# When the experts' weights are loaded: sixteen chunks ahead of the first tokens, the rest behind the experts' up-projections

## The chip, the core and the metric

The kernel runs on one core of one Trainium2 chip. The metric is device time in microseconds (us) of one execution, inputs and outputs in HBM. All of the work is in float32; TensorE's score matmuls take the fp32r form.

## What is computed

Attention with query pooling, and then a mixture of experts on its result. Cut to what matters:

```python
def _attn_ref(q, k, v):                 # q, k, v: 2 x 8 x 1152 x 64
    q_pool = q.reshape(B, H, S // 2, 2, D).mean(axis=3)
    scores = scale * np.matmul(q_pool, k.transpose(0, 1, 3, 2))
    attn = softmax(scores)              # written out in the reference
    return np.matmul(attn, v)

def _moe_ref(x, w_gate, w1, w2, capacity):   # x: 1152 x 512, 8 experts, F 1024, capacity 288
    logits = x @ w_gate
    expert_idx = np.argmax(logits, axis=1)
    gate_w = softmax(logits)[np.arange(N), expert_idx]
    # token i goes to the next free row of its expert while there is one
    h = np.maximum(np.einsum('ecd,edf->ecf', disp, w1), 0.0)
    y = np.einsum('ecf,efd->ecd', h, w2)
    out[i] = gate_w[i] * y[expert_idx[i], pos[i]]     # for the tokens that were kept
```

## The kernel before

**Attention** runs over eight pairs of heads (`rounds`, L686). PE makes scores (L371), transposes the exponentials (L409) and multiplies with the values (L434); the results are turned into token rows in `x_tok`, an SBUF tile of 1152 rows. `routing` (L488) picks each token's expert and scatters its row with an indirect DMA from Pool (L551) into `xs`, a buffer in HBM with 288 rows for each expert. The last five of these scatters come at the very end of attention. Behind them PE runs eight warm-up matmuls (L763, two passes each) on a tile that is already there.

**The expert stage** (L961 to L978) runs the eight experts in order. The order of the instructions is the written one on Pool, SP, ScalarE and PE (`manual_schedule(engines=MS)`).

- Tokens: `load_x(e)` (L791) brings the 288 rows of an expert from `xs` in three DMAs, into one of three buffers; for expert 0 SP issues them, for the others Pool. They can start when all scatters have landed. `trans_x` (L797) turns a block of 128 rows on PE.
- Units: an expert's rows are worked in up to four units of 64, 64, 128 and 32 rows. `unit(e, 0)` always runs. `later(e, 1)` (L948) is a branch (L950) on PE, ScalarE, VectorE and Pool, nested for the units behind it: each unit runs when the expert has that many tokens. SP has no part in the branches. Code of units that don't run is jumped over; `hint` marks for the engine, ahead of time, where a branch will be.
- A unit of 64 rows: 32 up-projection matmuls on PE (`up`, L890), ReLU on ScalarE and VectorE (L897, L895), two pairs of transposes (L904), 32 down-projection matmuls (L930), scaling on ScalarE (L822) and an indirect DMA to the output from Pool (L828). Units of 128 rows go through `block` (L849, L864).
- Weights: each expert has four chunks of 1 MB, two of `w1` and two of `w2`, 32 in all. `load_w(i)` (L608) loads chunk i from SP into buffer i mod 16 of `wraw`. Buffers 0 to 5 (`NR0`) have memory of their own and are loaded early in attention. Buffers 6 to 15 (L781) take over memory of attention's tiles, tile by tile: a load waits until the tiles under its buffer have been read for the last time. Chunks 6 to 12 (`NR1` is 13) go out before the tokens of expert 0, in the order of SP's queue, chunks 13 to 15 behind them. After expert e the four chunks from 4e + 16 follow, into the buffers that this expert has just given back.
- From chunk 15 on (`NR1 + AHEAD`) SP first reads a word of the chunk two before (L616), so that it waits until that one has landed: at most two loads are under way.

The instructions' own code is fetched by DMA as well: the page shows two queues of that kind, q8 with 32 packets of 16 KB and q14 with 25 smaller ones.

Of the kernel before, what the change touches and what calls it, by code (L numbers as in the profile page):

```python
# [20 lines left out]
EL = 3  # L21
PTB = (1, 1)
MS = {mybir.EngineType.Pool, mybir.EngineType.SP, mybir.EngineType.Activation, mybir.EngineType.PE}
NR, NR0, NR1 = 16, 6, 13
NX = 3
AHEAD = 2
ENG = [mybir.EngineType.PE, mybir.EngineType.Activation, mybir.EngineType.DVE, mybir.EngineType.Pool]
FAR = 1.0e6
UT = 2


def f32(ap):
    return ap.bitcast(F32)
# [3 lines left out]
def attention_moe(ctx: ExitStack, tc, cap, q, k, v, wg, w1, w2, out):  # L37
    nc = tc.nc
    B, H, S, D = q.shape
    SQ = S // 2  # L40
    E, DM, F = w1.shape
# [27 lines left out]
        out=upper, in_=f32(upper), compare_op=ALU.is_gt, fill=0.0, base=0,  # L69
# [20 lines left out]
    for j in range(2):  # L90
        nc.scalar.dma_start(
            out=wgi[j * D:(j + 1) * D, :, P + j * E:P + (j + 1) * E], in_=wg_r[j]
# [507 lines left out]
    wraw = [wraw_p.tile([P, 4, 512], F32, name=f"wraw{i}") for i in range(NR0)]  # L600
# [4 lines left out]
        for c in range(2):  # L605
            chunks.append((e, 1, c))

    def load_w(i):  # L608
        e, m, c = chunks[i]
        if m == 0:  # L610
            src = w1[e].rearrange("(a p) f -> p a f", p=P)[:, :, c * 512:(c + 1) * 512]
        else:
            src = w2[e, c * 512:(c + 1) * 512, :].rearrange("(a p) d -> p a d", p=P)
        if i >= NR1 + AHEAD:

            nc.values_load_multi_w_load_instructions(  # L616
                wraw[(i - AHEAD) % NR][0:1, 0, 0:1].bitcast(I32), engines=[mybir.EngineType.SP],
                skip_runtime_bounds_check_because="the value is not used",
            )
        nc.sync.dma_start(out=wraw[i % NR], in_=src)  # L620

    def posts_run(f):
        while f is not None:
# [167 lines left out]
    def load_x(e):  # L791
        q = nc.gpsimd if e else nc.sync
        for s, c in blocks:
            r = e * cap + s
            q.dma_start(out=xes[e % NX][0:c, s // P, :], in_=xs[r:r + c, :])

    def trans_x(e, b):  # L797
        xe, xf = xes[e % NX], xfs[e % 2]
        c = blocks[b][1]
        ps = tr_ps.tile([P, 512], F32, tag="tr", name="xps")  # L800
        for d in range(DC):
            nc.tensor.transpose(ps[:, d * c:(d + 1) * c], xe[0:c, b, d * P:(d + 1) * P], ident[0:c, 0:c])
        nc.scalar.copy(xf[:, :, b * P:b * P + c], ps[:, 0:DC * c].rearrange("p (d c) -> p d c", c=c))

    def tags(e, u):
        o, n = units[u]
        xe, gt, it = xes[e % NX], gts[e % 4], ids[e % 4]
        src, b = slice(o % P, o % P + n), o // P
        for g in range(1 if n == P else 2):
            rows = slice(g * n, (g + 1) * n)  # L810
            c = DM + 1 if n == P else DM + 2 + g
            nc.gpsimd.tensor_copy(gt[rows, u:u + 1], xe[src, b, DM:DM + 1])
            nc.gpsimd.tensor_copy(it[rows, u:u + 1], xe[src, b, c:c + 1].bitcast(I32))

    def send(e, u, ps):
        n = units[u][1]
        w = DM if n == P else DM // 2
        c = n * DM // w
        gate = gts[e % 4][0:c, u:u + 1]
        yo = y_p.tile([P, DM], F32, tag="yo", name="yo")  # L820
        if n >= D:
            nc.scalar.activation(yo[0:c, 0:w], ps[0:c, 0:w], AF.Copy, scale=gate)  # L822
        else:
            yq = y_p.tile([D, 256], F32, tag="yq", name="yq", bufs=1)
            nc.scalar.copy(yq[0:c], ps[c:2 * c, 0:256])
            nc.vector.tensor_tensor(out=yq[0:c], in0=ps[0:c, 0:256], in1=yq[0:c], op=ALU.add)
            nc.vector.tensor_scalar(out=yo[0:c, 0:w], in0=yq[0:c], scalar1=gate, scalar2=None, op0=ALU.mult)
        ins = nc.gpsimd.indirect_dma_start(  # L828
            out=out.rearrange("t (g d) -> (t g) d", d=w),
            out_offset=bass.IndirectOffsetOnAxis(ap=ids[e % 4][0:c, u:u + 1], axis=0),  # L830
            in_=yo[0:c, 0:w],
            in_offset=None,
            bounds_check=NTOK * DM // w - 1,
            oob_is_err=False,
        ).ins
        tc.declare_no_dep(ins, group="send", reason="each token has a row of its own")
        tc.add_to_no_dep_group("send", ins)
# [29 lines left out]
    def unit(e, u, between=(), hint=lambda: None):  # L867

        tags(e, u)
        o, n = units[u]  # L870
        if n == P:
            return block(e, u, between, hint)
        xf = xfs[e % 2]
        raw = [wraw[(4 * e + c) % NR] for c in range(4)]
        G = P // n
        Q = F // G // 256
        todo = list(between)

        def step():
            if todo:  # L880
                todo.pop(0)()

        def up(q):
            ps = h_ps.tile([P, 512], F32, tag="h", name="hps")
            for d in range(DC):
                if q and d == UT and not todo:
                    turn(0)
                for g in range(G):
                    c = g * (F // G) + q * 256
                    at = nc.tensor.matmul(  # L890
                        ps[g * n:(g + 1) * n, 0:256], xf[:, d, o:o + n], raw[c // 512][:, d, c % 512:c % 512 + 256],
                        start=d == 0, stop=d == DC - 1,
                    )
            if q:
                nc.vector.tensor_scalar_max(hs[:, q], ps[:, 0:256], 0.0)  # L895
            else:
                nc.scalar.activation(hs[:, q], ps[:, 0:256], AF.Relu)  # L897
            with tc.issue_after(at.ins):
                hint()

        def turn(q):
            ps = tr_ps.tile([P, 512], F32, tag="tr", name="htp")
            for j in range(2):
                nc.tensor.transpose(ps[:, j * P:(j + 1) * P], hs[:, q, j * P:(j + 1) * P], ident)  # L904
            dst = ht[:, 2 * q:2 * q + 2].rearrange("p j c -> p (j c)")
            if q or Q == 1:
                nc.vector.tensor_copy(dst, ps[:, 0:256])  # L907
            else:
                nc.scalar.copy(dst, ps[:, 0:256])  # L909

        held = Q == 2 and bool(todo)
        for q in range(Q):
            up(q)
        if held:
            turn(0)
        step()
        if held:
            turn(1)
        if Q == 1:
            turn(0)  # L920
        ps = y_ps.tile([P, 512], F32, tag="y", name="yps")
        U = G // 2
        NF = FC // U
        for i in range(NF):
            for w in range(U):
                j, g = divmod(i, 2) if U == 1 else (i % 2, 2 * w + i // 2)
                r = g * (F // G) + j * P
                for c in range(2):
                    k = (2 * w + c) * n
                    nc.tensor.matmul(  # L930
                        ps[k:k + n, 0:256], ht[:, j, g * n:(g + 1) * n],
                        raw[2 + r // 512][:, r % 512 // P, c * 256:(c + 1) * 256],
                        start=i == 0, stop=i == NF - 1,
                    )
            if i == 1 and Q == 2 and not held:
                turn(1)
            if i > 1:
                step()
        while todo:
            step()  # L940
        send(e, u, ps)

    def hint(e, u, flags):
        if u < NU:
            return lambda: tc.mark_branch_hint_location(f"u{e}_{u}", hint=flags[u - 1], engines=ENG)
        return lambda: None
# [9 lines left out]
    def flags_of(e):  # L956
        flags.append(nc.values_load_multi_w_load_instructions(
            more_i[0:1, e, :], engines=ENG, min_val=0, max_val=1, skip_runtime_bounds_check_because="each is the outcome of a comparison"
        )[1])

    with tc.manual_schedule(engines=MS):  # L961
        flags = []
        flags_of(0)
        for i in range(NR0, NR1):
            load_w(i)
        for e in range(min(NX, E)):
            load_x(e)
        for i in range(NR1, min(NR, 4 * E)):
            load_w(i)
        trans_x(0, 0)  # L970
        for e in range(E):
            nxt = [lambda: trans_x(e + 1, 0), lambda: flags_of(e + 1)] if e + 1 < E else ()
            unit(e, 0, nxt, hint(e, 1, flags[e]))
            later(e, 1, flags[e])
            if e + NX < E:
                load_x(e + NX)
            for i in range(4 * e + NR, min(4 * e + NR + 4, 4 * E)):
                load_w(i)  # L978


# [23 lines left out]
```

## Time and profile before

| | us |
|---|---|
| median of 3 runs | 491.99 |
| lowest and highest | 490.84, 493.25 |
| the profiled execution, its time | 491.99 |
| the profiled execution, its span | 490.3 |
| mean granted clock of TensorE | 0.974 |
| bytes read from and written to HBM | 52.48 MB, 11.98 MB |

The span runs from the first to the last instruction; all times below are counted from its start. PE is TensorE's matmul, PEld its weight load, PEq its sequencer; DVE is VectorE, ACT ScalarE, POOL GpSimd, SP SyncE, and a name with a q at its end is that engine's sequencer. A line such as L890 is a line of the kernel. `A <- B` reads "A waited, and B released it". [...] The attention takes the first 300 us, the expert stage the rest.

### The profile page before, as it was taken

The numbers are of one execution on the slowest core, as the hardware profiler recorded it, in microseconds if no ns is written. First come the engines' busy times: TensorE is split into PE (matmuls) and PEld (weight loads), VectorE is DVE, ScalarE is ACT, GpSimd is POOL, SyncE is SP. The second block draws the span as 40 slices with busy tenths as digits, with TensorE's granted clock in tenths as the row PEclk, the third lists the DMA queues.
The fourth block names the chain that finished last, engine by engine and source line by source line (L and its number), as shares of the span: only waits on it lengthen the run. The fifth ranks groups of instructions, "written<-read, shape, count | busy, mean of one in ns | idle before, by whom it ended". The sixth has DMA issues, their size and how long they took to land. (4 is left out here: it accounts for less than half of the span.)

```text
span 490.3 us, 9116 instructions
## 1 busy us (share of the span) xinstructions
PE 449.8 (92%) x3183; PEld 315.5 (64%) x3183; DVE 245.9 (50%) x725; ACT 251.1 (51%) x731; POOL 170.9 (35%) x290
## 2 busy tenths in 40 slices
PE   4779999999999999999999998996999999999990
PEld 3667777777677677677776765464668456674670
DVE  5687777777777999887777565010100011001100
ACT  5777887787787677777777761020221112101100
POOL 4477444344344454454433001522031133112110
PEclk9799999999999999999999999798999999999996
DMA  7998984033043044052104625699983093000000
GB/s 216 276 284 282 385 285 108 5 98 100 5 98 102 1 119 124 3 150 55 30 20 139 260 70 204 215 341 355 363 285 145 5 364 123 13 12 24 12 11 21
DMA packets 55737, 69.96 MB, mean 143 GB/s; under 512 B 21873, under 2 KB 32117, under 8 KB 55680
## 3 DMA queue, kind: packets, MB, share of 16 engines
q1 hardware_dynamic: 50320, 53.56, 35.5%
q0 software_dynamic: 4816, 15.66, 8.5%
q8 instruction: 32, 0.52, 0.4%
q14 instruction: 25, 0.20, 0.1%
q10 hardware_dynamic: 544, 0.02, 0.1%
HBM read 52.48 MB, written 11.98 MB: 131 GB/s over the span
## 5 line engine op out<-in xcount | busy, mean ns | idle before, releaser
L376 DVE TENSOR_REDUCE negm<-s 128x1 f32<-128x384 f32 x216 | 119.6, 554 | 56.9 <-PE s L371 55.8
L371 PE MATMUL s<-k,q 128*128 128x384 f32 x432 | 132.8, 390 | 9.6 <-ACT p L392 9.0
L392 ACT ACTIVATE p<-s,negm 128x384 f32<-128x384 f32 x216 | 125.0, 587 | 14.6 <-DVE negm L380 9.2
L409 PE MATMUL tp<-ident,p 128*128 128x128 f32 x648 | 106.8, 274 | 0.5 <-DVE pt L418 0.4
L371 PEld LDWEIGHTS s<-k,q 128*128 128x128 f32 x432 | 66.8, 194 | 45.3 <-ACT p L392 25.2
L409 PEld LDWEIGHTS tp<-ident,p 128*128 128x128 f32 x648 | 83.9, 141 | 10.0 <-issue 1.4
L420 ACT COPY pt<-tp 128x384 f32<-128x384 f32 (+1 forms) x160 | 69.3, 445 | 38.5 <-PE tp L409 35.5
L434 PE MATMUL pv<-pt,vraw 128*64 128x256 f32 (+2 forms) x612 | 85.4, 403 | 0.8 <-ACT xt L442 0.8
L273 POOL TENSOR_TENSOR q<-qts,q 64x256 fp32r<-64x256 f32 (+1 forms) x76 | 52.0, 693 | 55.0 <-DVE q L267 47.8
L229 POOL TENSOR_TENSOR k<-kts,k 64x384 fp32r<-64x384 f32 x42 | 44.8, 1068 | 53.7 <-DVE k L228 51.9
L890 PE MATMUL hps<-wraw,xf 128*64 128x256 f32 (+1 forms) x448 | 49.7, 390 | 8.1 <-PEq L950 4.6
L828 POOL DMA_INDIRECT out_dram<-yo,id x17 | 17.1, 1006 | 112.9 <-issue 42.5
L434 PEld LDWEIGHTS pv<-pt,vraw 128*64 128x64 f32 x612 | 36.3, 136 | 27.2 <-issue 10.6
L930 PE MATMUL yps<-wraw,ht 128*64 128x256 f32 (+1 forms) x448 | 48.1, 382 | 1.2 <-DVE ht L907 1.2
L895 DVE TENSOR_SCALAR hs<-hps 128x256 f32<-128x256 f32 x12 | 5.1, 425 | 87.9 <-PE hps L890 87.9
L890 PEld LDWEIGHTS hps<-wraw,xf 128*64 128x64 f32 (+1 forms) x448 | 30.5, 136 | 26.5 <-issue 7.5
L392 ACT ACTIVATION_READ_ACCUMULATOR p<-s,negm 128x1 f32 x216 | 44.5, 206 | 0.0
L418 DVE COPY pt<-tp 128x384 f32<-128x384 f32 (+1 forms) x80 | 40.0, 508 | 6.1 <-PE tp L409 6.0
L822 ACT ACTIVATE yo<-yps,gt 128x256 f32<-128x256 f32 (+1 forms) x15 | 7.7, 516 | 61.5 <-PE yps L930 31.1
L930 PEld LDWEIGHTS yps<-wraw,ht 128*64 128x64 f32 (+1 forms) x448 | 28.4, 133 | 16.8 <-ACT ht L909 1.8
L849 PEld LDWEIGHTS hps<-xf,wraw 128*128 128x128 f32 x192 | 21.7, 192 | 1.2 <-issue 1.2
L849 PE MATMUL hps<-xf,wraw 128*128 128x128 f32 x192 | 22.2, 277 | 0.0
(117 smaller groups left out, 377.0 us busy)
## 6 DMA issues: line engine op xcount, KB each, us to landing
wraw<-in_moe_w_dram SPq DMA_DIRECT2D x32, 1024.0 KB, 7.9
vraw<-in_v_dram SPq DMA_DIRECT2D x8, 576.0 KB, 4.0
kc<-k SPq DMA_DIRECT2D x16, 288.0 KB, 4.0
xs<-zrow POOLq DMA_DIRECT2D x4, 1032.0 KB
qraw<-in_q_dram SPq DMA_DIRECT2D x16, 256.0 KB, 3.6
kraw<-in_k_dram SPq DMA_DIRECT2D x14, 288.0 KB, 4.6
xe<-xs POOLq DMA_DIRECT2D x14, 258.0 KB, 6.0
out_dram<-zrow POOLq DMA_DIRECT2D x2, 1024.0 KB
```

The costliest lines, as they stand in the source:

```text
L229: nc.gpsimd.tensor_tensor(out=tl[rl, c], in0=kt_s[rh, :], in1=f32(tl[rh, c]), op=ALU.subtract)
L273: nc.gpsimd.tensor_tensor(out=tl[r0, 1, c], in0=qt_s[rs, a:z], in1=f32(tl[rs, 0, c]), op=ALU.subtract)
L371: nc.tensor.matmul(ps[:, 0:CW], a, w, start=i == 0, stop=i == len(terms) - 1)
L376: nc.vector.tensor_reduce(out=negm3[g][:, j:j + 1], in_=ps[:, 0:CW], axis=AX.X, op=ALU.max, negate=True)
L392: nc.scalar.activation(pexp[g][:, j * CW:(j + 1) * CW], sthird.pop(n)[:, 0:CW], AF.Exp, bias=negm3[g][:, 3:4], scale=1.0, accum_out=sums[p ...
L409: nc.tensor.transpose(ps[:, i * P:(i + 1) * P], pexp[g][:, kt * P:(kt + 1) * P], ident)
L418: nc.vector.tensor_copy(dst, sr)
L420: nc.scalar.copy(dst, sr)
L434: nc.tensor.matmul(ps[j * D:(j + 1) * D, 0:n], vraw[:, j, kt, :], pts[p, j, src][:, kt, c0:c0 + n], start=kt == 0, stop=kt == KT - 1,)
L849: at = nc.tensor.matmul(ps[:, i * n:(i + 1) * n], raw[c][:, d, i * P:(i + 1) * P], xf[:, d, o:o + n], start=d == 0, stop=d == DC - 1,)
L890: at = nc.tensor.matmul(ps[g * n:(g + 1) * n, 0:256], xf[:, d, o:o + n], raw[c // 512][:, d, c % 512:c % 512 + 256], start=d == 0, stop=d ...
L930: nc.tensor.matmul(ps[k:k + n, 0:256], ht[:, j, g * n:(g + 1) * n], raw[2 + r // 512][:, r % 512 // P, c * 256:(c + 1) * 256], start=i == ...
```

## The change

Three things change in the expert stage. `NR1` becomes 16, so that chunks 6 to 15 all go out on SP ahead of the tokens of expert 0. The loads behind an expert move up: they are issued between its first unit and its branch, as far as a table says (`UPTO`): none at expert 0, two at expert 1 (16 and 17), three each at 2 and 3, four each at 4 and 5. And each of these loads waits for a matmul of its expert: the last one of the first half of unit 0's up-projections (`unit` now returns it). The wait for the chunk two before starts at chunk 18 instead of 15.

```diff
-NR, NR0, NR1 = 16, 6, 13
+NR, NR0, NR1 = 16, 6, 16
+UPTO = (16, 18, 21, 24, 28, 32)
...
-    def load_w(i):
+    def load_w(i, behind=None):
...
-        nc.sync.dma_start(out=wraw[i % NR], in_=src)
+        ins = nc.sync.dma_start(out=wraw[i % NR], in_=src).ins
+        if behind is not None:
+            tc.add_manual_dep(
+                ins, behind.name, mybir.DependencyInfo(mybir.DependencyClass.Sync, mybir.DependencyReason.DATA),
+                reason="loads follow the experts",
+            )
...
             with tc.issue_after(at.ins):
                 hint()
+            return at.ins
...
-        for q in range(Q):
-            up(q)
+        ats = [up(q) for q in range(Q)]
...
         send(e, u, ps)
+        return ats[0]
...
         for e in range(min(NX, E)):
             load_x(e)
-        for i in range(NR1, min(NR, 4 * E)):
-            load_w(i)
+        sent = NR1
         trans_x(0, 0)
         for e in range(E):
             nxt = [lambda: trans_x(e + 1, 0), lambda: flags_of(e + 1)] if e + 1 < E else ()
-            unit(e, 0, nxt, hint(e, 1, flags[e]))
+            at = unit(e, 0, nxt, hint(e, 1, flags[e]))
+            while sent < min(4 * E, UPTO[min(e, len(UPTO) - 1)]):
+                load_w(sent, behind=at)
+                sent += 1
             later(e, 1, flags[e])
             if e + NX < E:
                 load_x(e + NX)
-            for i in range(4 * e + NR, min(4 * e + NR + 4, 4 * E)):
-                load_w(i)
```

## Rows read from the trace of the kernel before

**Rows 1.** The page: its first line and PE's line of busy time.
```profile
span 490.3 us, 9116 instructions
PE 449.8 (92%) x3183; PEld 315.5 (64%) x3183; DVE 245.9 (50%) x725; ACT 251.1 (51%) x731; POOL 170.9 (35%) x290
```

**Rows 2.** Timeline of PE from 300 us on: start, length, line, idle time before.
```profile
299.79 1.01 PE L434 MATMUL pv<-pt,vraw 128*64 128x64 f32 x28
315.33 0.60 PE L802 MATMUL xps<-ident,xe 128*128 128x128 f32 x4
325.64 3.67 PE L890 MATMUL hps<-wraw,xf 128*64 128x256 f32 x32 [0.69 <-ACTq L950]
338.52 5.36 PE L890 MATMUL hps<-wraw,xf 128*64 128x256 f32 x32 [4.58 <-PEq L950]
402.79 3.67 PE L890 MATMUL hps<-wraw,xf 128*64 128x256 f32 x32 [0.67 <-ACTq L950]
411.76 3.67 PE L890 MATMUL hps<-wraw,xf 128*64 128x256 f32 x32 [0.67 <-ACTq L950]
```

**Rows 3.** Who PE waited for, 300 us to the end: total, times, longest.
```profile
PE hps L890 <- PEq L950: 4.6, 1, 4.6
PE hps L890 <- ACTq L950: 2.8, 4, 0.7
```

**Rows 4.** The branch, line 950, on PE at three exits: ns, start.
```profile
L950 PEldq COMPARE_BRANCH  x1: 6457/6457/6457, 331.6 to 331.6; - x1
...
L950 PEldq COMPARE_BRANCH  x1: 1031/1031/1031, 399.8 to 399.8; - x1
...
L950 PEldq COMPARE_BRANCH  x1: 2529/2529/2529, 408.8 to 408.8; - x1
```

**Rows 5.** DMA queues in 331.7 to 335.5, 334.9 to 336.9, 408.8 to 410: packets, MB, share.
```profile
q1 hardware_dynamic: 507, 1.02, 78.7%
...
q8 instruction: 1, 0.02, 3.5%
...
q8 instruction: 1, 0.02, 5.5%
```

**Rows 6.** Busy time by stretch; last columns granted clock, DMA share, GB/s.
```profile
304.00:311.00 7.00, 6.53 (x12) 3.29 (x12) 2.17 (x24) 0.21 (x1) 4.86 (x5) 0.55 0.36 139
338.50:342.00 3.50, 3.48 (x18) 2.54 (x20) 0.00 (x0) 0.00 (x0) 1.66 (x6) 0.54 0.89 290
360.00:372.00 12.00, 12.00 (x108) 8.03 (x106) 1.70 (x4) 2.77 (x6) 3.31 (x8) 1.00 1.00 358
401.60:402.80 1.20, 0.53 (x8) 0.08 (x4) 0.00 (x0) 0.47 (x1) 0.00 (x0) 1.00 1.02 392
410.60:411.80 1.20, 0.53 (x8) 0.08 (x4) 0.00 (x0) 0.47 (x1) 0.00 (x0) 1.00 0.00 0
```

**Rows 7.** Timeline of SP's DMA issues, 280 to 314 us.
```profile
289.96 10.03 SPq L620 DMA_DIRECT2D wraw<-in_moe_w_dram  x3
311.95 1.29 SPq L795 DMA_DIRECT2D xe<-xs  x3
313.29 0.97 SPq L620 DMA_DIRECT2D wraw<-in_moe_w_dram  x2
```

**Rows 8.** Timeline of Pool: the last scatter.
```profile
309.51 0.91 POOL L551 DMA_INDIRECT xs<-x_tok,slot  x1 [0.30 <-issue]
```

**Rows 9.** Landing: L828 in 410:470, 390:405; L795 in 311:312.3, 327:332.
```profile
DMA to landing us min/median/max: 2.4/2.4/2.4
...
DMA to landing us min/median/max: 4.9/4.9/4.9
...
DMA to landing us min/median/max: 2.7/2.7/2.7
...
DMA to landing us min/median/max: 5.7/5.7/5.7
```

**Rows 10.** DMA queue of SP in 299 to 304.4 us: packets, MB, share.
```profile
q1 hardware_dynamic: 528, 1.05, 61.2%
```

## The prediction

> **What bounds the kernel now.** I read the page first: PE is busy for 92% of the span [rows 1], so an idle stretch of PE is time to be won, and a new one is time lost. Next comes PE's timeline in the expert stage, where the change works: the last matmuls of attention, the first transposes of expert 0's tokens at 315.33 us with warm-up matmuls right up to them, and then one expert after another [rows 2]. I call the experts e0 to e7 and the chunks of weights load 0 to load 31, four for each expert. Experts 0, 1, 4 and 5 run unit 0 alone and jump over their other units. The waits of PE in this stage have one large row: 4.6 us once, released by PE's own sequencer at the branch, against 2.8 us over four other jumps, 0.7 each [rows 3]. The large one is e1's exit, before e2's first matmul at 338.52 [rows 2]. The branch rows tell why: e1's branch took 6.5 us on PE's sequencer, e4's 1.0 and e5's 2.5 [rows 4]. A branch of 2.5 us is almost covered, because it starts while the last 2 us of the expert's matmuls are still to run.
>
> The DMA view shows what the long one waited for: between 331.7 and 335.5 no packet of PE's instruction queue ran while weights took 79% of the 16 engines, and the one packet of 16 KB stands in the next stretch; the branch ends 338.1, behind it. At e5's exit, with the weights done, the packet comes within 1.2 us of the branch [rows 4, 5]. So weights in flight delayed e1's code. [...]
>
> Ahead of all this lies one more chain: scatters of tokens leave Pool about 1.2 us apart, the last at 309.51; when it has landed (about 311.9), SP issues e0's tokens, 2.7 us later the first block is there, and PE turns it at 315.33 [rows 2, 7 to 9]. The DMA engines are busy for a third of that time [rows 6]; load 12 goes out at 299.6 and is over by 304.4, loads 13 and 14 go out behind e0's tokens at 313.3 [rows 7, 10].
>
> **The change part by part.**
>
> *Loads 13 to 15 move ahead of e0's tokens.* On SP's queue they pass the load of e0's tokens; on Pool's nothing moves. What holds them? By the order and size of the pools in the code, buffers 13 to 15 lie over the second p tile and the pt tiles of attention, whose last readers are the transposes that released load 12 and the matmuls of L434, over at 300.8 [rows 2]. So the three loads leave at 300 to 301, 13 us or more earlier, and the scatters of x_tok run beside them. Bytes: from 304.4 on there are three loads of 1.05 MB and about 1.2 MB of scatters, 4.3 MB. At 358 GB/s, the rate of a saturated stretch [rows 6], they need 12.1 us, to 316.5. e0's tokens are in SP's queue behind load 15, so their first block (0.26 MB, 0.7 us, and the landing) is there no sooner than about 317.3, against 314.7: 2.6 us, all of it on the path, since the warm-up of PE ends at 315.3 and nothing else is ready. Bounds: 0, if scatters and tokens get through as now; and 6 us, if the last scatter takes 4.9 us where a store of this kind alone takes 2.4, and the tokens behind it 5.7 where they took 2.7 [rows 9], 2.5 and 3.0, rounded up for the place in the queue. I take 2.6, by the bytes. PE is then idle for 3 us or more; after the idle 4.6 us at e1's exit the clock was at the lower level, which cost 1.7 us, and after the 0.7 us at e4's it was not [rows 2, 3, 6]. Between 0 and 1.7 I take half, 0.9. Sum: +3.5.
>
> The trace shows the sharing: stores of rows land in 2.4 us alone and in 4.9 us beside weights [rows 9]. [...] Were there separate paths instead, the +3.5 would be 0.
>
> *No weights between load 15 and e1's first up-projection.* From about 317 to 327.7 the DMA engines carry the tokens of e1 and e2 alone. e0's exit is at its floor already (0.7 us): 0.
>
> *Loads 16 and 17 behind e1's first up-projection.* The matmul named is half-way through the 3.67 us of up-projections that begin at 325.64 [rows 2], so they leave at about 327.6 and move data about 1 us later. e1's branch comes at 331.6 [rows 4], 4 us after the release. e1's own next page of code finds a quiet DMA. If the jump's target is fetched before the two loads or between them, the exit falls to the 0.7 us of the others: 4.6 - 0.7 = 3.9, and the 1.7 us of slow clock with it: -5.6. If it is fetched behind both, the stall stays: 0. I take -5.6, since in the trace the packet came when a load that had been in flight at the branch was over, and now one of only two loads has 3 us of head start.
>
> That rests on when a busy engine serves the code. The row: from the branch at 331.6 no packet until 335.5, with weights and tokens filling the engines [rows 4, 5]. [...]
>
> *Later loads.* Loads 18 to 23 follow e2 and e3 and land far ahead of use. Loads 24 to 27 now wait for e4's first up-projection. e5 takes 9.0 us (402.79 to 411.76 [rows 2]), so e4 starts near 393.8 and the release is near 395.8; 28 to 31 follow e5's, near 404.8. Eight loads, 8.4 MB at 358 GB/s, keep the engines full from 396 to 420. e6 needs the first two at 411.76; by then 16 us of transfer have passed, five loads' worth: 0, with 8 us of cover; were that gone, PE would wait for the rest one to one. But e5's exit, which now has a DMA share of 0 beside it [rows 6], will meet weights. Its branch of 2.5 us just fits; a delay of its page adds one to one. Bounds: 0, as at e4's exit, which has weights beside it (share 1.02) and a branch of 1.0 us [rows 4, 6]; +5.6, e1's stall over again. Nearer to e4's: +0.8.
>
> *Waits added on SP.* Behind each such wait only later loads are queued on SP; the tokens of e1 to e7 are Pool's. The matmul waited for already signals ScalarE. Loads 15 to 17 lose their wait for the load two before them. 0.
>
> **Sum.** +3.5 - 5.6 + 0.8 = -1.3. The profiled execution took 491.99 us, 490.3 of span [rows 1] and 1.7 around it, and is the median of the three runs (490.84 to 493.25). 491.99 - 1.3 = 490.7 us.
>
> **The rivals.**
> *Start hidden.* The tokens come on time, because the scatters are limited by their issue (about 1.2 us apart [rows 8]) and the loads have drained by then. Then only -5.6 + 0.8 or so counts: 486.4 to 489.4. For it: a DMA share of 0.36 in those 7 us [rows 6]. Against it: the bytes above.
> *The wait moves (slower).* The first block of tokens pays both contended landings and the slow clock (+6 + 1.7), and e5's exit takes part of e1's stall (+2 to +3); e1's exit still gives -5.6. That is 496 to 497 in full, and 491.5 with half of each. It decides when the last scatter is served behind load 15 instead of ahead of it.
> *e1's stall stays.* The code's page is served behind loads 16 and 17, so nothing is won there: with +2.6 to +4.3 at the start, 494.6 to 496.3. For it: at 331.6 two loads and e3's tokens are in flight, as now. It is also the case in which spacing the loads out does nothing.
>
> **How the numbers follow.** The forecast (start later by 2 to 4.5 us, e1's stall gone) spans 488.7 to 492.5 and gets 0.42; start hidden 0.24; the wait moves 0.22; stall stays 0.12. About 0.5% (2.5 us) is what a measurement of this kernel can tell from no change, so faster means below 489.5, slower above 494.5. Faster: 0.24 and 0.11 of the forecast's, 0.35. Slower: 0.15 of the moved wait and 0.10 of the stall that stays, 0.25. Same: 0.40. The range takes in all cases up to the full moved wait: 486.5 to 497. Cases of either sign hold most of the chance, so the forecast's own range stands beside it: 488.7 to 492.5.
>
> **What would show it.** Loads 13 to 15 at 300 to 301 on SP. The first transposes of e0 later than 315.33: 317 to 318 by the forecast, 315.5 if hidden, above 319 if the wait moved; the last scatter's landing tells which term. e1's branch: 2.5 us or less and a wait of 0.7, with a clock of 1.00 behind it, or again 6 us. e5's branch: 2.5 us, or more. What would make it wrong outright: loads 13 to 15 leaving no sooner than before, or PE waiting for weights of e6.

## The result

The changed kernel takes 498.2 us (median of 4 runs, 497.45 to 498.79), the kernel before 491.41 us beside it (489.95 to 493.25): a ratio of 1.0149, 95% interval 1.0112 to 1.0186. It is slower by about 7 us; 490.7 was forecast, with a range of 486.5 to 497. Executions of one kernel lie up to 7.6 us apart here, in part for a reason that the experiments show, so the comparisons below rest on medians of 4 to 12 executions and, above all, on the steps that a trace shows. Of the runs called both and warm11 one execution each, more than 1.5% above the fastest, counts in the median and not in the ratio.

The page of the changed kernel, its first line and the busy times, answers to [rows 1]:

```profile
span 497.0 us, 9104 instructions
PE 452.8 (91%) x3183; PEld 316.3 (64%) x3183; DVE 243.7 (49%) x725; ACT 251.1 (51%) x731; POOL 171.0 (34%) x290
```

The span grew by 6.7 us. PE's timeline (start, length, what, idle time before; the up-projections are now L896, the branch L957) answers to [rows 2]:

```profile
317.67 0.92 PE L808 MATMUL xps<-ident,xe 128*128 128x128 f32 x4 [2.52 <-DMA xe<-xs]
319.31 6.33 PE L896 MATMUL hps<-wraw,xf 128*64 128x256 f32 x32 [0.72 <-ACT xf L809]
330.97 3.67 PE L896 MATMUL hps<-wraw,xf 128*64 128x256 f32 x32 [0.69 <-ACTq L957]
339.94 3.67 PE L896 MATMUL hps<-wraw,xf 128*64 128x256 f32 x32 [0.67 <-ACTq L957]
402.43 3.67 PE L896 MATMUL hps<-wraw,xf 128*64 128x256 f32 x32 [0.67 <-ACTq L957]
416.50 5.54 PE L896 MATMUL hps<-wraw,xf 128*64 128x256 f32 x32 [5.77 <-PEq L957]
```

Three places differ. e0's first transposes waited 2.52 us for tokens, and e0's up-projections took 6.33 us where they took 3.67 before. e2 begins 0.67 us behind e1, so e1's exit is cured, with a granted clock of 1.00 behind it (340 to 343.6). e6 begins after 5.77 us of idle time, and takes 5.54 us: e1's stall of before, larger, at e5's exit. The waits of PE say the same in sums (compare [rows 3]):

```profile
PE hps L896 <- PEq L957: 5.8, 1, 5.8
PE hps L896 <- ACTq L957: 2.7, 4, 0.7
PE xps L808 <- DMA xe<-xs: 2.5, 1, 2.5
```

The branch on PE at the exits of e1, e4 and e5 (ns, start), as in [rows 4]:

```profile
L957 PEldq COMPARE_BRANCH  x1: 340/340/340, 337.0 to 337.0; - x1
...
L957 PEldq COMPARE_BRANCH  x1: 349/349/349, 399.5 to 399.5; - x1
...
L957 PEldq COMPARE_BRANCH  x1: 7650/7650/7650, 408.4 to 408.4; - x1
```

The DMA queues, as in [rows 5] (packets, MB, share of the 16 engines), in 331.5 to 332.94, 408.5 to 413.5 and 413.5 to 414.7 us:

```profile
q8 instruction: 1, 0.02, 6.2%
...
q1 hardware_dynamic: 802, 1.61, 93.8%
...
q8 instruction: 1, 0.02, 5.8%
```

At e1 the 16 KB of code were on their way before loads 16 and 17 left (332.95 below). At e5 the branch came at 408.4, no packet of code ran for 5 us while weights had 94% of the engines, and then the one packet came; PE went on 1.8 us after it was over. The stretches, as in [rows 6] (the last three columns are granted clock, DMA share, GB/s):

```profile
304.00:311.00 7.00, 6.61 (x10) 3.17 (x11) 1.94 (x21) 0.21 (x1) 4.83 (x5) 0.52 1.04 354
315.20:317.60 2.40, 0.00 (x0) 0.00 (x0) 0.00 (x0) 0.00 (x0) 2.18 (x4) 1.00 0.64 191
317.90:324.70 6.80, 6.08 (x30) 3.40 (x30) 0.00 (x0) 0.97 (x2) 1.39 (x6) 0.50 0.52 182
411.20:416.50 5.30, 0.00 (x0) 0.03 (x1) 0.00 (x0) 0.10 (x1) 1.65 (x5) 0.72 0.95 310
416.50:420.30 3.80, 3.80 (x18) 2.40 (x20) 0.00 (x0) 0.02 (x1) 0.00 (x0) 0.50 0.78 268
```

In the first row the DMA share is 1.04 where it was 0.36; in the third and the fifth the clock is at its lower level, 0.50 of full speed, both times behind an idle PE (2.52 and 5.77 us). SP's issues, as in [rows 7], and the landing of the scatters and of e0's first block alone, the latter as in [rows 9]:

```profile
289.67 11.82 SPq L621 DMA_DIRECT2D wraw<-in_moe_w_dram  x6
314.99 1.29 SPq L801 DMA_DIRECT2D xe<-xs  x3
332.95 11.26 SPq L621 DMA_DIRECT2D wraw<-in_moe_w_dram  x4
395.45 26.17 SPq L621 DMA_DIRECT2D wraw<-in_moe_w_dram  x8
```

```profile
DMA to landing us min/median/max: 5.7/6.9/8.0
...
DMA to landing us min/median/max: 2.6/2.6/2.6
```

Loads 10 to 15 leave from 289.67 to 301.5, as the prediction had it. The five scatters landed 5.7 to 8.0 us after their issue, the last one 5.7, where about 2.4 lay between the last issue and SP's tokens before [rows 7, 8]; SP sent e0's tokens at 314.99 instead of 311.95; their first block took its usual 2.6 us.

The span's difference adds up from these rows, in us, changed kernel less the one before:

| step | us |
|---|---|
| attention ends earlier (the last L524, L523 before, at 304.39 for 304.69) | -0.30 |
| e0's up-projections start at 319.31 for 316.65, without that | +2.96 |
| e0's up-projections 6.33 for 3.67 | +2.66 |
| e1's exit 0.67 for 4.58 | -3.91 |
| e2's up-projections 3.67 for 5.36 | -1.69 |
| e5's exit 5.77 for 0.67 | +5.10 |
| e6's up-projections 5.54 for 3.67 | +1.87 |
| sum | +6.69 |

### The profile page after: what moved, and what is told of

Same layout as the page of the kernel before. It is cut to its first block, busy times and chain, and to the rows that moved or that the text cites. A ratio compares the mean times of both kernels' runs of the same rounds, so it can differ in the third digit from the quotient of the medians.

```text
span 497.0 us, 9104 instructions
## 1 busy us (share of the span) xinstructions
PE 452.8 (91%) x3183; PEld 316.3 (64%) x3183; DVE 243.7 (49%) x725; ACT 251.1 (51%) x731; POOL 171.0 (34%) x290
## 5 line engine op out<-in xcount | busy, mean ns | idle before, releaser
L896 PE MATMUL hps<-wraw,xf 128*64 128x256 f32 (+1 forms) x448 | 52.5, 406 | 9.2 <-PEq L957 5.8
L896 PEld LDWEIGHTS hps<-wraw,xf 128*64 128x64 f32 (+1 forms) x448 | 31.4, 142 | 29.7 <-issue 12.3
L828 ACT ACTIVATE yo<-yps,gt 128x256 f32<-128x256 f32 (+1 forms) x15 | 7.7, 516 | 61.5 <-PE yps L936 27.8
```

The costliest lines, as they stand in the source:

```text
L896: at = nc.tensor.matmul(ps[g * n:(g + 1) * n, 0:256], xf[:, d, o:o + n], raw[c // 512][:, d, c % 512:c % 512 + 256], start=d == 0, stop=d ...
```

## The experiments

The theory after the result: the change trades one stall for two. Three loads beside the scatters, called the head from here on, hold up e0's tokens (+5.6 with the slow clock behind the idle time), weights at e5's exit hold up PE's code (+7.0), and e1's exit is cured (-5.6). The rivals are told with each run. Ratios are to the kernel before, beside it on the same chip, with 95% intervals.

| run | median us | ratio | interval |
|---|---|---|---|
| no_head | 496.06 | 1.0130 | 1.0036 to 1.0223 |
| head_alone | 493.49 | 1.0044 | 1.0006 to 1.0083 |
| quiet_arrival | 497.33 | 1.0115 | 1.0020 to 1.0211 |
| both | 494.59 | 1.0064 | 1.0021 to 1.0107 |
| no_late_13 | 485.87 | 0.9893 | 0.9863 to 0.9923 |
| no_late_16 | 492.35 | 1.0014 | 0.9984 to 1.0044 |
| one_ahead | 496.73 | 1.0123 | 1.0048 to 1.0198 |
| quarters | 499.93 | 1.0193 | 1.0108 to 1.0278 |
| spaced | 487.73 | 0.9946 | 0.9917 to 0.9975 |
| warm11 | 493.57 | 1.0066 | 1.0027 to 1.0105 |
| quiet_exit | 493.51 | 1.0042 | 1.0014 to 1.0070 |

### What weights at the exits cost, and what the head costs by itself

Two edits of the kernel before, both without loads 16 to 31: no_late_13, and no_late_16 with the three loads ahead of e0's tokens.

```diff
-            for i in range(4 * e + NR, min(4 * e + NR + 4, 4 * E)):
-                load_w(i)
```

and, in no_late_16 beside that,

```diff
-NR, NR0, NR1 = 16, 6, 13
+NR, NR0, NR1 = 16, 6, 16
```

> The kernel before without loads 16 to 31: experts 4 to 7 work with the weights that lie in the buffers of experts 0 to 3 (that part of the computation is changed). Theory: with no weights in flight after load 15 every exit is quiet from e1 or e2 on; loads 13 to 15 are over by 329, before e1's branch at 331.6, so e1's exit waits 0.7 us and the clock behind it is 1.00: 491.4 - 5.6 = 485.8. Rival: the stall at e1's exit doesn't come from weights in flight; then it stays at 4 to 5 us and the time near 491.

> As no_late_13, with loads 13 to 15 ahead of e0's tokens; so the two differ by the head alone, with no weights behind it. Theory: the head costs 5.6 us by itself (tokens 2.95 later, and 2.67 of slow clock in e0's up-projections), here as in the changed kernel: 485.8 + 5.6 = 491.4. Rival: the delay of the tokens is partly won back later in the stage, by loads that no longer run beside e0 and e1; then the two differ by 3 us or less.

Measured: 485.87 us (485.14 to 486.20, 8 runs) and 492.35 (490.61 to 493.61, 10 runs). PE's timeline of the first, at e0, e2 and e6:

```profile
314.69 0.66 PE L802 MATMUL xps<-ident,xe 128*128 128x128 f32 x4 [0.89 <-DMA xe<-xs]
316.07 3.67 PE L890 MATMUL hps<-wraw,xf 128*64 128x256 f32 x32 [0.72 <-ACT xf L803]
334.03 3.67 PE L890 MATMUL hps<-wraw,xf 128*64 128x256 f32 x32 [0.67 <-ACTq L950]
405.49 3.67 PE L890 MATMUL hps<-wraw,xf 128*64 128x256 f32 x32 [0.67 <-ACTq L950]
```

and of the second:

```profile
317.72 1.11 PE L802 MATMUL xps<-ident,xe 128*128 128x128 f32 x4 [3.39 <-DMA xe<-xs]
319.55 5.71 PE L890 MATMUL hps<-wraw,xf 128*64 128x256 f32 x32 [0.72 <-ACT xf L803]
339.54 3.67 PE L890 MATMUL hps<-wraw,xf 128*64 128x256 f32 x32 [0.67 <-ACTq L950]
411.00 3.67 PE L890 MATMUL hps<-wraw,xf 128*64 128x256 f32 x32 [0.67 <-ACTq L950]
```

Without these weights every exit waits 0.67 to 0.69 us, and the time falls to 485.87 where 485.8 was expected, 5.2 us below the median of the kernel before beside it (491.04). In the rows the two steps that were e1's stall and its slow clock give 5.6. That settles where the stall of the kernel before came from. It also takes most of the spread with it: 8 runs within 1.1 us, where the kernel before beside them spread over 6.6 (487.89 to 494.53). So most of the spread hangs on the late loads; that it is pages of code that come early or late is argued from the traces, one for each kernel. With the head the spread is 3.0 us again.

These runs show one thing more, the time of a branch beside quiet engines. In no_late_16 it took 2473 ns at e1's exit; at e4's and e5's:

```profile
L950 PEldq COMPARE_BRANCH  x1: 361/361/361, 399.1 to 399.1; - x1
...
L950 PEldq COMPARE_BRANCH  x1: 2503/2503/2503, 408.0 to 408.0; - x1
```

So e1's and e5's exits take 2.5 us here without any weights, just covered by the matmuls that are still to run, and a packet of code starts within 0.3 us of either branch. At e4's exit no packet runs beside the branch. In the kernel before and in the changed one the packet of 16 KB next to that branch was over ahead of it, too: it ran from 398.2 to 399.4 and from 394.8 to 395.8, with the branch at 399.8 and 399.5. So weights had something to delay at e1's and e5's exits, and nothing at e4's. In no_late_13 e1's branch took 2.32 us and e5's 0.53, so a page can be there early too.

The head alone then costs 6.5 us, of which nothing is won back; 5.6 were expected. Its rows: an idle 3.39 us ahead of the first transposes instead of 0.89, and e0's up-projections at 5.71 us instead of 3.67.

### One half of the change at a time

The changed kernel with loads 13 to 15 back behind e0's tokens (no_head):

> The changed kernel, but loads 13 to 15 go out behind e0's tokens, as in the kernel before. Theory: the three loads beside the scatters cost 5.6 us at the start, 2.95 by the later tokens (last scatter landing 5.7 us instead of 2.3) and 2.67 by the clock at its lower level in e0's up-projections; without them e0's first transposes stand at about 315.3 and its up-projections take 3.67 us, and e1's and e5's exits stay as in the changed kernel (0.7 and about 5.8 us): 498.2 - 5.6 = 492.6. Rival: the delay of the start is made up elsewhere, because e1's exit is quiet only thanks to loads 13 to 15 being over by 317; then e1's exit shows 4 to 5 us again and the time stays at 497 to 498.

```diff
-        for i in range(NR0, NR1):
+        for i in range(NR0, NR1 - 3):
             load_w(i)
         for e in range(min(NX, E)):
             load_x(e)
+        for i in range(NR1 - 3, NR1):
+            load_w(i)
```

Measured: 496.06 us (493.93 to 499.76, 4 runs). PE at e0, e2 and e6:

```profile
316.48 3.67 PE L896 MATMUL hps<-wraw,xf 128*64 128x256 f32 x32 [0.72 <-ACT xf L809]
336.62 3.67 PE L896 MATMUL hps<-wraw,xf 128*64 128x256 f32 x32 [2.83 <-PEq L957]
411.67 6.34 PE L896 MATMUL hps<-wraw,xf 128*64 128x256 f32 x32 [4.27 <-PEq L957]
```

The start is on time and e0's up-projections are back at 3.67 us, as the theory has it. But e1's exit, which the theory left cured, waited 2.83 us: the rival was half right. The median is 2 us below the changed kernel's and not 5.6, and with four executions from 493.93 to 499.76 that is no clear difference. Loads 13 to 15 now ran until 329, and loads 16 and 17, issued at 327.5 and 327.9, were in flight at the branch at 331.5; which of them held up e1's code this run doesn't tell.

The kernel before with the first half of the change alone (head_alone):

> The kernel before, with loads 13 to 15 ahead of e0's tokens and nothing else of the change (loads 16 and on leave when their buffers are free, with the wait for the load two before from 18 on). Theory: the start is later by 5.6 us; loads 16 and 17 leave at e0's exit, ahead of the fetch of e1's jump target, so that e1's exit stalls for 4 us and more as in the kernel before; e5's exit is quiet: 491.4 + 5.6 = 497.0. Rival: e1's exit was cured by the quiet engines from 317 on and not by the added wait; then it shows 0.7 us here too and the time is about 491.4.

```diff
-NR, NR0, NR1 = 16, 6, 13
+NR, NR0, NR1 = 16, 6, 16
```

Measured: 493.49 us (490.56 to 496.68, 10 runs). PE at e0, e2 and e6:

```profile
318.62 6.07 PE L890 MATMUL hps<-wraw,xf 128*64 128x256 f32 x32 [0.72 <-ACT xf L803]
338.99 3.67 PE L890 MATMUL hps<-wraw,xf 128*64 128x256 f32 x32 [0.67 <-ACTq L950]
413.14 3.67 PE L890 MATMUL hps<-wraw,xf 128*64 128x256 f32 x32 [1.72 <-PEq L950]
```

The theory was wrong here: e1's exit is cured without any added wait. The time lies between the two expectations, 2 us above the rival's, since e5's exit waited 1.72 us and PE stood for 1.41 us in the middle of e3's first up-projections, where the profile shows nothing that it waited for. So the wait for the up-projection is not what cures e1's exit. Engines that carry few weights when PE arrives at e1 aren't enough either: quiet_arrival and quiet_exit below have the same head and still waited there for 2.83 and 3.19 us. And the head costs more than the cure brings.

### Which weights e5's exit waits for

`UPTO` says up to which load SP has gone behind the first up-projection of e0, e1 and so on. The edits here and in the next two parts are made to the changed kernel.

First the table of quiet_arrival:

> The changed kernel with another table: loads 24 to 27 follow e3's first up-projection instead of e4's, so that the engines carry no weights when PE arrives at e5; 28 to 31 follow e5's as in the changed kernel and are in flight at e5's exit. [...] With a quiet arrival the target is fetched ahead of loads 28 and 29, e5's branch takes under 1 us and the wait at its exit 0.7, with a granted clock of 1.00 behind it: 498.2 - 7.0 = 491.2. Rival: what counts is that weights are in flight at the branch itself; then e5's exit still shows 4 to 6 us and the time stays within 1 us of 498.2.

```diff
-UPTO = (16, 18, 21, 24, 28, 32)
+UPTO = (16, 18, 21, 28, 28, 32)
```

Measured: 497.33 us (493.97 to 499.93, 4 runs). PE at e2 and e6:

```profile
342.45 5.17 PE L896 MATMUL hps<-wraw,xf 128*64 128x256 f32 x32 [2.83 <-PEq L957]
417.43 5.22 PE L896 MATMUL hps<-wraw,xf 128*64 128x256 f32 x32 [2.69 <-PEq L957]
```

The idea fell that a quiet arrival is enough: with loads 28 and 29 behind e5's first up-projection its exit still waited 2.69 us, and e6's up-projections took 5.22 us behind it. That this is half of the 5.77 can't be put down to the edit: warm11 below, with the table of the changed kernel, waited 2.75 us there. The time stayed, as the rival has it, but there was a second cause: e1's exit, untouched by this edit, waited 2.83 us in this execution.

Then that of quiet_exit:

> The changed kernel with loads 24 to 27 behind e3 and 28 to 31 behind e6, so that no weights are in flight at e4's and e5's exits; head and loads 16 to 23 as changed. Theory: the loads at e5's exit alone cost 7.0 us (5.1 of wait and 1.87 of slow clock) in the changed kernel; here e5's exit waits 0.7 us, e6's up-projections take 3.67 us and the time is 498.2 - 7.0 = 491.2, plus what e1's exit takes in an execution in which its page is late (0 to 5.6, so 491 to 494). Rival: e5's wait is of another cause, or goes to e4's or e6's units; then 497 to 498.

```diff
-UPTO = (16, 18, 21, 24, 28, 32)
+UPTO = (16, 18, 21, 28, 28, 28, 32)
```

Measured: 493.51 us (491.81 to 495.17, 12 runs), 4.7 us below the changed kernel. PE at e2 and e6:

```profile
341.54 5.00 PE L896 MATMUL hps<-wraw,xf 128*64 128x256 f32 x32 [3.19 <-PEq L957]
414.41 3.67 PE L896 MATMUL hps<-wraw,xf 128*64 128x256 f32 x32 [0.76 <-ACTq L957]
```

With no weights near it, e5's exit waits 0.76 us and e6's up-projections take 3.67. The loads at e5's exit were the cause of the 7.0 us. What is left over the 491.2 of the expectation is put down to e1's exit, 3.19 us here with 5.00 us of up-projections behind it.

The two edits of no_head and quiet_arrival together (both):

> The last but one and the one before together: loads 13 to 15 behind e0's tokens, loads 24 to 27 behind e3, 28 to 31 behind e5. Theory: both losses go and the gain at e1's exit stays: 498.2 - 5.6 - 7.0 = 485.6, which beats the kernel before by 5.8 us. Rival: one of the two stays as told above: 491 to 493, no better than the kernel before.

Measured: 494.59 us (491.16 to 498.72, 10 runs), 9 us above the expectation. The profiled execution was the longest of the ten, so its rows show the worst case and not the median. Both exits stalled in it, as e2 and e6 tell:

```profile
337.15 6.41 PE L896 MATMUL hps<-wraw,xf 128*64 128x256 f32 x32 [4.55 <-PEq L957]
415.57 6.45 PE L896 MATMUL hps<-wraw,xf 128*64 128x256 f32 x32 [4.90 <-PEq L957]
```

### How a page of code stands in line

The first run, one_ahead:

> The changed kernel with one load under way instead of two: from load 17 on SP waits for the load just before. Theory: a page of code waits for what is queued on its engine at the time, the rest of a load and a whole one behind it, 5.1 us at e5's exit; with one load under way it is the rest of one, 0 to 3 us, and the wait at e5's exit falls from 5.8 to between 0.7 and 3.5 us, with no slow clock behind it: 498.2 - 4 = 494, if no expert waits for weights. Rival: the delay is of the busy engines as such, however little is queued; then e5's branch still takes 6 us or more and the time stays at 498.

```diff
-AHEAD = 2
+AHEAD = 1
```

Measured: 496.73 us (495.53 to 499.73, 4 runs). PE at e2 and e6:

```profile
340.68 3.67 PE L896 MATMUL hps<-wraw,xf 128*64 128x256 f32 x32 [1.85 <-PEq L957]
415.66 5.36 PE L896 MATMUL hps<-wraw,xf 128*64 128x256 f32 x32 [4.19 <-PEq L957]
```

A partial miss: the wait at e5's exit fell from 5.77 to 4.19 us, and not to 3.5 or less. One load under way is enough for a stall. What the second adds isn't shown: with two under way the same exit waited from 2.75 us (warm11) to 5.77.

The second, quarters:

> The changed kernel with loads 16 to 31 each cut into four DMAs of 256 KB, as many bytes under way as before. Rival mechanisms for the page of code: it is served at the end of the DMA in flight (then quarters serve it within 1 us, e5's exit waits under 2 us and the time falls to 492 or so), or behind all that is queued on the engine (then e5's exit still waits 4 to 6 us and the time stays within 1.5 us of 498.2). Theory: the second, since at e5's exit the page came only after the load that was still queued at the branch.

```diff
-        ins = nc.sync.dma_start(out=wraw[i % NR], in_=src).ins
+        for j in range(4) if i >= 16 else (slice(0, 4),):
+            ins = nc.sync.dma_start(out=wraw[i % NR][:, j], in_=src[:, j]).ins
...
```

Measured: 499.93 us (496.81 to 502.86, 4 runs). PE at e2 and e6:

```profile
340.13 3.67 PE L897 MATMUL hps<-wraw,xf 128*64 128x256 f32 x32 [0.67 <-ACTq L958]
415.37 6.09 PE L897 MATMUL hps<-wraw,xf 128*64 128x256 f32 x32 [4.45 <-PEq L958]
```

As expected: with DMAs of a quarter of the size and as many bytes under way e5's exit waits 4.45 us, and not under 2. So the code doesn't wait just for the end of the DMA in flight. The median lies 1.7 us above the 498.2, a little more than the 1.5 allowed for.

### The clock at the start

This is warm11:

> The changed kernel with eleven warm-up matmuls instead of eight, so that PE is busy until e0's tokens land near 317.6. Theory: the lower clock in e0's up-projections (6.33 us for what takes 3.67) comes from the idle 2.5 us ahead of them; without that idle time it goes, the up-projections take 3.67 us and the first transposes stay near 317.7: 498.2 - 2.7 = 495.5. Rival: the clock falls there whatever PE does just before; then 6 us and 498 again, or 498 to 500 if the warm-up now ends behind the tokens.

```diff
-        for _ in range(8):
+        for _ in range(11):
             nc.tensor.matmul(warm[:, 0:512], ident, wraw[0][:, 0], start=True, stop=True)
```

Measured: 493.57 us (490.75 to 498.36, 10 runs). PE at e0's transposes, e0 and e6:

```profile
316.88 0.66 PE L808 MATMUL xps<-ident,xe 128*128 128x128 f32 x4 [1.67 <-DMA xe<-xs]
318.26 3.67 PE L896 MATMUL hps<-wraw,xf 128*64 128x256 f32 x32 [0.72 <-ACT xf L809]
409.76 5.20 PE L896 MATMUL hps<-wraw,xf 128*64 128x256 f32 x32 [2.75 <-PEq L957]
```

With 1.67 us of idle time instead of 2.52 ahead of the tokens, e0's up-projections take 3.67 us: the slow clock there depends on what PE does just before, as the theory has it, and the rival falls. The edit adds work and shortens the idle time at once, so it doesn't tell the two apart. The other traces, all with eight warm-up matmuls, speak for the idle time: with 2.5 to 4.5 us of it (seven traces) e0's up-projections took 5.7 to 6.3 us, with 0.9 or less (five) 3.67. The median fell by 4.6 us where 2.7 were expected; e5's exit waited 2.75 us in this execution, not 5.77, and that part of the fall isn't the warm-up's doing.

### A version with the loads away from the exits

This is spaced:

> All of the computation, with the loads where no expert is jumped out of: loads 13 to 15 behind e0's tokens, as in the kernel before; 16 to 23 behind e2's first up-projection, 24 to 27 behind e3's, 28 to 31 behind e6's, with the wait that the change added. Theory: e1's, e4's and e5's exits wait 0.7 us each, the tokens of e0 come on time and no expert waits for weights (e4 needs load 16 near 388, e7 load 28 near 442): about 486, as the kernel without those loads (485.9), and faster than both kernels. Rival: the losses move once more, to e2's or e3's pages of code or to late weights; then 489 to 492.

It is no_head with another table:

```diff
-UPTO = (16, 18, 21, 24, 28, 32)
+UPTO = (16, 16, 24, 28, 28, 28, 32)
```

Measured: 487.73 us (486.51 to 491.63, 12 runs) against 490.45 beside it: a ratio of 0.9946, interval 0.9917 to 0.9975: faster than the kernel before by half a percent, and than the changed kernel by about 10 us. PE at e0, e2 and e6:

```profile
315.75 3.67 PE L896 MATMUL hps<-wraw,xf 128*64 128x256 f32 x32 [0.72 <-ACT xf L809]
334.65 3.67 PE L896 MATMUL hps<-wraw,xf 128*64 128x256 f32 x32 [1.60 <-PEq L957]
407.30 3.67 PE L896 MATMUL hps<-wraw,xf 128*64 128x256 f32 x32 [0.67 <-ACTq L957]
```

The start is on time, e5's exit quiet, and no expert waits for weights. e1's exit still waited 1.60 us here, with loads 13 to 15 as the only weights sent out behind e0's tokens by then, and PE stood for 0.97 us in the middle of e3's first up-projections. These two are about the 1.9 us by which it misses the kernel without the late loads. The loads aren't away from every jump: e2 too is left by one, behind its second unit, with 16 to 23 sent out ahead of it; that exit waited 0.67 us.

## Why the prediction was wrong

- *What bounds the kernel*: right. The stall at e1's exit was a page of code behind weights, and its price 5.6 us: taking the weights away gave 5.6 in the rows and 5.2 in the medians (no_late_13).
- *Loads 13 to 15*: the issue times were right, and so was the thought that weights hold up the start. The delay was 2.96 us where 2.6 were taken, and that it came so close is luck. The sum by bytes let e0's tokens wait in SP's queue behind load 15; but when they left, at 314.99, the engines had almost run dry (DMA share 0.11 from 315 to 316), and their first block took its usual 2.6 us. It was the scatters that held up the tokens: the last one landed 5.7 us after its issue instead of 2.4, 3.3 us more. That term stood only in the upper bound, with 2.5; 0.7 of it was hidden, since before the tokens lay ready while the warm-up ran on, and the slow clock in the first transposes added 0.3. The clock was mis-sized: "I take half, 0.9" between 0 and 1.7; it cost 2.66, more than the upper end, because the lower level lasted 6.8 us and not the 3.5 us seen behind e1's stall. With the longer warm-up e0's up-projections took 3.67 us again.
- *Loads 16 and 17*: -5.6 was measured, in this execution. That is luck too: the reason given, the head start over two loads that wait, isn't what did it. head_alone has no such wait and the same cure; quiet_arrival, quiet_exit and one_ahead have the wait and stalled for 1.9 to 3.2 us.
- *Later loads*: this step failed and turned the sign. The weights arrived in time for e6, as worked out. But "nearer to e4's: +0.8" took e4's exit as the model for e5's, and 7.0 us came, 1.4 more than the upper end of 5.6. The prediction's own rows told the two exits apart: with no weights beside it e5's branch took 2.5 us and a packet of code ran within 1.2 us of it, while e4's took 1.0 [rows 4, 5]. no_late_16 shows the same, 2.50 and 0.36. e5's branch took 2.4 us or more in twelve of the thirteen traces, and a packet of code began behind the branch, 0.1 us in the kernel before, 5.2 in the changed one with weights beside it; at e4's the packet was over ahead of the branch in both, and its exit waited 0.67 us in all thirteen traces, with weights beside it or without. e1 and e5 are reached by a jump, e4 by running through e3's units; that this makes the difference fits, but no run tested it. The model had to be e1's exit, which was in the rows; then the sum is +3.5 - 5.6 + 5.6 = +3.5, and with the measured clock 5.3, and the forecast is "slower".
- *Waits added on SP*: 0, right.
- *The rivals*: "the wait moves", with 0.22 and 496 to 497, had the sign and nearly the time, but other terms: the start cost 5.6 us and not 7.7, since only the scatters paid for the weights, and e5's exit 7.0 and not 2 to 3. Its condition wasn't met either: the last scatter landed at 314.9, load 15 at 316.0. Measured were 498.2, 1.2 above the end of the range (497.0), which the clock's excess at e0 alone (1.8 over the 0.9 taken) outweighs. "Start hidden" is refuted by no_late_16. "e1's stall stays" is not what this trace shows, but it came true in part in three kernels that issue the same loads up to that exit (quiet_arrival, quiet_exit, one_ahead).

Open: why a page is there ahead of e1's branch in some executions (changed kernel, quarters, warm11, head_alone) and not in others of the same order (quiet_arrival, quiet_exit, one_ahead). Quiet engines don't decide it, for in no_late_16, with no weights at all, e1's branch took 2.47 us. The runs show the outcomes, not the rule. Nor did they show what the fetch does with the branch hints.

## What to carry to other kernels

Where branches jump over code, look at how long each branch takes beside quiet engines: keep bulk loads away from those that fetch a page (here 2.5 us, at e1's and e5's exits), and judge a stall that you move by an exit of that kind, not by one that merely has weights beside it. DMA engines that looked idle just ahead of a critical small transfer weren't free here: three loads beside five scatters cost 6.5 us with nothing won, where the prediction's sum had 3.5, and part of it because PE's clock fell with the wait. And when one kernel's executions differ by over 1%, look in the traces for pages of code that come early or late before trusting a median of three.

## What the runs showed of the hardware

- Beside weights a page of code came late even where each DMA was small. Over the 2.5 us of a quiet branch, e5's took 5.1 us more with two loads of 1 MB under way (7.65), 3.6 with one (6.07), and 3.8 with as many bytes as two in quarters (6.33). That fits a page that waits for what is queued when it is asked for, and speaks against one that waits for a single DMA. How the delay grows with what is queued isn't shown: with two loads under way it was 2.1 us in warm11 (4.64).
- In exits with a branch of 2.5 us and more PE's wait is the length of the branch less about 1.9 us: 7.65 and 5.77 (changed kernel, e5), 6.46 and 4.58 (before, e1), 6.07 and 4.19 (one_ahead, e5), 2.53 and 0.67 (before, e5). Shorter branches left the wait at 0.67 (0.34 and 0.35 in the changed kernel, 1.03 before). So the branch's row prices the wait, but not the clock behind it.
- Behind 2.52 us of idle time the granted clock was 0.50 for 6.8 us (317.9 to 324.7), longer than the idle time itself; behind 1.67 us, after a longer warm-up, the up-projections took 3.67 us in warm11, as long as e2's in the changed kernel, where the clock was 1.00. The length of the wait alone doesn't settle it: 2.83 us at e1's exit were followed by up-projections of 3.67 us in no_head and of 5.17 in quiet_arrival.
